# Requesting the q weights ahead of x tile 3, and four more products of zeros ahead of the first transposes

## The chip, the cores and the metric

One NeuronCore of one Trainium2 chip runs the kernel. The metric is device time in microseconds (us) of one execution, lower is better. A profiled execution also has a span, counted from the first instruction; it is about 1.7 us shorter than the time. Times inside a trace below count from the span's start.

## The reference, cut to what matters

One transformer-like block on x of 2048 rows by 512 columns (bf16): layer norm; a local, dilated attention over q, k and v; a gated feed-forward part; x plus the product of the two.

```python
xn = _layernorm(x, axis=-1)
s = _A_ref(xn, A_wqkv, A_wo)          # qkv = xn @ wqkv, attention over 8 positions, @ wo
g = _silu(_B_ref(xn, B_w_gate, B_w_up, B_w_down))
return x + s * g
```

Only the start matters here. To form the first q product the kernel needs two tiles of x (tile 0 and tile 1, 128 rows each), normalized and transposed, and the q third of wqkv.

## The kernel before

All loads are asked for by SyncE, on one queue, in the order of the program: the first four x tiles (128 KB each), then the q, k and v weights (512 KB each), then the rest.

```python
for t in range(TPQ):                  # TPQ = 4
    load_x(t)
for i in range(3):
    load_w(wqkv_sb, A_wqkv, i * D, (i + 1) * D)
load_x(TPQ, TPQ)
... # gate and up weights, further x tiles
```

While the first x tile is on its way TensorE multiplies zeros ("warm_up"), whose results nobody reads; they keep the array active. Tile 0 and tile 1 are then normalized on VectorE, transposed on TensorE into PSUM and copied to SBUF on ScalarE.

```python
warm_up(17, TQ // 2)                  # 17 products of 256 columns of zeros
first_moments(0)                      # VectorE: statistics; ScalarE: square root
first_moments(1)
first_normalize(0)
transpose(0)                          # TensorE x4, then one copy by ScalarE
first_normalize(1)
warm_up(4, P)                         # 4 products of 128 columns of zeros
transpose(1, parts=2)                 # TensorE x4, then two copies by ScalarE
warm_up(4, P)
first_moments(2)
first_moments(3)                      # needs x tile 3
first_normalize(2)                    # behind the statistics of tile 3 on VectorE
first_normalize(3)
... # 16 products for q over tiles 0 and 1; transposes of tiles 2 and 3; k, v
```

The softmax here doesn't subtract the row's maximum and nothing guards it: scores larger than these inputs give would overflow.

Of the kernel before, what the change touches and what calls it, by code (L numbers as in the profile page):

```python
# [13 lines left out]
P = 128  # L14
# [14 lines left out]
def kernel(  # L29
# [14 lines left out]
    B, S, D = A_x.shape  # L44
    DF = B_w_gate.shape[1]
    NT, NC, NF, NJ = S // P, D // P, DF // P, S // TQ
    TPQ = TQ // P
# [27 lines left out]
    wqkv_sb = wts.tile([P, NC, 3 * D], BF16, name="wqkv_sb")  # L75
# [6 lines left out]
    def load_x(t, n=1):  # L82
        nc.sync.dma_start(
            out=x_sb[:, t : t + n, :],
            in_=x2d[t * P : (t + n) * P, :].rearrange("(t p) d -> p t d", p=P),
        )

    def load_w(dst, src, lo, hi):
        nc.sync.dma_start(
            out=dst[:, :, lo:hi], in_=src.rearrange("(k p) n -> p k n", p=P)[:, :, lo:hi]  # L90
        )

    for t in range(TPQ):
        load_x(t)
    for i in range(3):
        load_w(wqkv_sb, A_wqkv, i * D, (i + 1) * D)
    load_x(TPQ, TPQ)
    for i, (lo, hi) in enumerate(((0, DF // 2), (DF // 2, DF))):
# [76 lines left out]
    def first_moments(t):  # L175
        nc.vector.bn_stats(out=stats[:, t, :], in_=x_sb[:, t, :])  # L176
        nc.vector.bn_aggr(out=mv[:, t, :], in_=stats[:, t, :])
        nc.scalar.activation(
            out=std[:, t, :], in_=mv[:, t, 1:2], func=AF.Sqrt, bias=epsc[:], scale=1.0
        )  # L180
# [39 lines left out]
    def warm_up(n, cols):  # L220

        ps = mm.tile([P, TQ], F32, name="warm_ps", tag="mm")
        for _ in range(n):
            nc.tensor.matmul(
                ps[:, 0:cols], lhsT=warm[:, 0:P], rhs=warm[:, 0:cols], start=True, stop=True
            )
# [240 lines left out]
    HT = TPQ // 2  # L467
    HQ = HT * P
    warm_up(17, TQ // 2)
    first_moments(0)  # L470
    first_moments(1)
    first_normalize(0)
# [72 lines left out]
```

## Time and profile before

| | before |
|---|---|
| time, median of 3 | 231.71 us (231.36 to 231.92) |
| span of the profiled execution | 229.8 us |
| TensorE busy | 98% |
| TensorE's share of the chain that ended last | 95% |
| first q product starts | 7.06 us |

The chain is followed back from the last instruction to whatever released it. A share of 95% for TensorE says that time can be gained elsewhere only where TensorE waits. Between its first product at 1.11 and the end of its last at 226.31, nearly all of that waiting is ahead of 7.06. The lines are in the prediction.

### The profile page before, as it was taken

Reading aid. Unit: us, or ns where it says so; the run is one execution under the profiler, and the core shown is the slowest. Engines: PE = TensorE matmul, PEld = TensorE weight load, DVE = VectorE, ACT = ScalarE, POOL = GpSimd, SP = SyncE. Lnnn points to the kernel's source line nnn. Section 1 sums busy time; section 2 is a strip of 40 time slices with the busy share of each in tenths; the row PEclk is TensorE's granted clock in tenths of the full one; section 3 lists DMA queues with packets and bytes.
Section 4 is the critical chain, followed back from the end, with each engine's and each line's share of the span. In section 5 each row is a group of like instructions: output and inputs, shape, how many; then the busy total and the mean of one; then the engine's idle time right before and its main releaser. Section 6 shows DMA issues by size and latency. Waiting matters only on the chain.

```text
span 229.8 us, 3547 instructions
## 1 busy us (share of the span) xinstructions
PE 224.7 (98%) x1339; PEld 107.6 (47%) x1339; DVE 147.5 (64%) x234; ACT 132.3 (58%) x219; POOL 20.9 (9%) x61
## 2 busy tenths in 40 slices
PE   7999999999999999999999999999999999999993
PEld 5865444444444444444444444444444444444453
DVE  5593896896995198865678169725449429945232
ACT  3779779765514867476721687646741387647211
POOL 1058924100000000110000000000000000000000
PEclk9999999999999999999999999999999999999998
DMA  6999499921288211100267611100047810000001
GB/s 156 365 374 372 109 205 200 301 81 49 85 182 198 62 27 24 26 0 0 93 163 162 146 30 23 27 11 0 27 138 160 204 30 0 0 0 4 23 23 46
DMA packets 27057, 23.71 MB, mean 103 GB/s; under 512 B 6688, under 2 KB 27040, under 8 KB 27040
## 3 DMA queue, kind: packets, MB, share of 16 engines
q1 hardware_dynamic: 27040, 23.49, 39.1%
q8 instruction: 10, 0.16, 0.3%
q14 instruction: 7, 0.06, 0.1%
HBM read 18.22 MB, written 4.21 MB: 98 GB/s over the span
## 4 chain that ended last, share of the span: by engine, by line
PE 95%; ACT 1%; DVE 1%; DMA 1%; issue 0%; DVEq 0%
PE y_ps L399 21%; PE u_ps L241 21%; PE g_ps L241 21%; PE qkv_ps L241 17%; PE s_ps L409 6%; PE L_ps L298 3%; PE o_ps L358 3%; DMA x_sb<-in_A_x_dram 1%; PE tr L207 1%; PE q_ps L241 1%; DVE stats L176 1%; ACT L383 1%; PE den_ps L318 0%; PE sp_ps L333 0%; ACT xnT L216 0%; ACT ge L383 0%
## 5 line engine op out<-in xcount | busy, mean ns | idle before, releaser
L241 PE MATMUL g_ps<-xnT,wg_sb 128*128 128x512 bf16 x224 | 57.6, 379 | 0.0
L241 PE MATMUL u_ps<-xnT,wu_sb 128*128 128x512 bf16 x224 | 57.5, 379 | 0.0
L399 PE MATMUL y_ps<-wd_sb,h 128*128 128x512 bf16 (+1 forms) x238 | 51.2, 366 | 0.0
L387 DVE TENSOR_TENSOR h<-ge,u 128x512 bf16<-128x512 bf16 x56 | 23.7, 424 | 36.6 <-ACT u L385 36.2
L287 DVE TENSOR_TENSOR pk<-q_sb,k_sb 128x2048 bf16<-128x2048 bf16 x32 | 37.8, 1220 | 8.8 <-ACT k_sb L262 8.8
L385 ACT ACTIVATE u<-u_ps 128x512 bf16<-128x512 f32 x56 | 33.5, 598 | 14.6 <-PE u_ps L241 14.5
L383 ACT ACTIVATE ge<-g_ps 128x512 bf16<-128x512 f32 x56 | 33.6, 599 | 14.0 <-PE g_ps L241 13.7
L241 PE MATMUL qkv_ps<-xnT,wqkv_sb 128*128 128x512 bf16 (+1 forms) x208 | 41.1, 355 | 0.0
L344 DVE TENSOR_TENSOR pv<-E,v_arr 128x2048 bf16<-128x2048 bf16 x32 | 38.6, 1216 | 0.0
L399 PEld LDWEIGHTS <-h 128*128 128x128 bf16 x238 | 23.3, 98 | 25.3
L406 ACT ACTIVATE sl<-y_ps 128x512 bf16<-128x512 f32 (+1 forms) x17 | 9.7, 572 | 44.0 <-PE y_ps L399 44.0
L241 PEld LDWEIGHTS <-wu_sb 128*128 128x128 bf16 x224 | 21.9, 98 | 26.6 <-issue 0.3
L241 PEld LDWEIGHTS <-wg_sb 128*128 128x128 bf16 x224 | 21.0, 98 | 26.1 <-issue 3.0
L241 PEld LDWEIGHTS <-wqkv_sb 128*128 128x128 bf16 x224 | 21.6, 98 | 19.5 <-issue 0.4
L417 DVE TENSOR_TENSOR m<-s_ps,sl 128x512 bf16<-128x512 f32 (+1 forms) x17 | 11.2, 657 | 24.2 <-PE s_ps L409 24.2
L409 PE MATMUL s_ps<-wo_sb,oT 128*128 128x512 bf16 (+1 forms) x68 | 16.6, 366 | 0.0
L192 POOL TENSOR_TENSOR rstd<-rstd,mhalf 128x1 f32<-128x1 f32 x12 | 7.7, 638 | 80.4 <-DVE rstd L189 78.2
L265 ACT ACTIVATE vst<-qkv_ps 128x512 bf16<-128x512 f32 x16 | 9.6, 597 | 6.2 <-PE qkv_ps L241 6.2
L262 ACT ACTIVATE k_sb<-qkv_ps 128x512 bf16<-128x512 f32 (+1 forms) x20 | 10.2, 516 | 3.5 <-PE qkv_ps L241 3.2
L370 DVE TENSOR_TENSOR oT<-o_ps,rb 128x1024 bf16<-128x1024 f32 x8 | 9.4, 1216 | 2.1 <-PE o_ps L358 2.1
L259 ACT ACTIVATE q_sb<-qkv_ps 128x512 bf16<-128x512 f32 (+1 forms) x16 | 8.7, 544 | 3.6 <-PE qkv_ps L241 3.3
L409 PEld LDWEIGHTS <-oT 128*128 128x128 bf16 x68 | 6.7, 98 | 7.2
(51 smaller groups left out, 120.9 us busy)
## 6 DMA issues: line engine op xcount, KB each, us to landing
v_arr<-vT SPq DMA_DIRECT2D x16, 520.0 KB, 5.2
vT<-vst SPq DMA_DIRECT2D x16, 128.0 KB, 1.7
out_dram<-o_t SPq DMA_DIRECT2D x15, 128.0 KB, 2.3
wg_sb<-in_B_w_gate_dram SPq DMA_DIRECT2D x2, 896.0 KB
wu_sb<-in_B_w_up_dram SPq DMA_DIRECT2D x2, 896.0 KB, 13.5
wd_sb<-in_B_w_down_dram SPq DMA_DIRECT2D x1, 1792.0 KB, 17.1
wqkv_sb<-in_A_wqkv_dram SPq DMA_DIRECT2D x3, 512.0 KB, 5.3
x_sb<-in_A_x_dram SPq DMA_DIRECT2D x3, 512.0 KB, 10.0
```

The source lines that it names most:

```text
L241: nc.tensor.matmul(ps, lhsT=w[:, dk, lo : lo + P], rhs=xnT[j][:, dk, i0 : i0 + n], start=(dk == 0), stop=(dk == NC - 1),)
L262: nc.scalar.activation(out=k_sb[:, c, lo : lo + n], in_=ps, func=AF.Copy)
L265: nc.scalar.activation(out=vst[:], in_=ps, func=AF.Copy)
L287: nc.vector.tensor_tensor(out=pk[:], in0=st[j]["q"][:], in1=k_sb[:, :, off : off + TQ], op=ALU.mult)
L344: nc.vector.tensor_tensor(out=pv[:], in0=st[j]["E"][:, wh, :].unsqueeze(1).to_broadcast([P, 4, TQ]), in1=st[j]["va"][:, 4 * g : 4 * g + 4, ...
L383: nc.scalar.activation(out=ge[:], in_=g_ps[:], func=AF.Gelu_apprx_tanh)
L385: nc.scalar.activation(out=u[:], in_=u_ps[:], func=AF.Copy)
L387: nc.vector.tensor_tensor(out=h[:], in0=ge[:], in1=u[:], op=ALU.mult)
L399: nc.tensor.matmul(y[:], lhsT=st[j][fc][:, tt * P : (tt + 1) * P], rhs=wd_sb[:, fc, cols], start=(fc == 0), stop=(fc == NF - 1),)
L406: nc.scalar.activation(out=sl[:, cols], in_=y[:], func=AF.Silu)
L409: nc.tensor.matmul(s[:], lhsT=st[j]["oT"][:, g, tt * P : (tt + 1) * P], rhs=wo_sb[:, g, cols], start=(g == 0), stop=(g == NC - 1),)
L417: nc.vector.tensor_tensor(out=m[:], in0=s[:], in1=sl[:, cols], op=ALU.mult)
```

## The change

The intent: let the q weights land before TensorE asks for them, and let TensorE have no idle piece between the seventeen products of zeros and the first transposes.

```diff
-    for t in range(TPQ):
+    for t in range(TPQ - 1):
         load_x(t)
-    for i in range(3):
+    load_w(wqkv_sb, A_wqkv, 0, D)
+    load_x(TPQ - 1)
+    for i in range(1, 3):
         load_w(wqkv_sb, A_wqkv, i * D, (i + 1) * D)
...
     warm_up(17, TQ // 2)
+    warm_up(4, P)
     first_moments(0)
```

## The prediction

> **What bounds the kernel now.** I read the page first: which engine is busy, then which chain ended last.
>
> ```profile
> span 229.8 us, 3547 instructions
> PE 224.7 (98%) x1339; PEld 107.6 (47%) x1339; DVE 147.5 (64%) x234; ACT 132.3 (58%) x219; POOL 20.9 (9%) x61
> ...
> PE 95%; ACT 1%; DVE 1%; DMA 1%; issue 0%; DVEq 0%
> ```
>
> TensorE is on the chain for 95% of the span; all other engines together hold about 5%. The changed code lies in the first 9 us, so the next view is the chain of waits in order of time, cut to that stretch (columns: start in us, length in us, what).
>
> ```profile
> 0.80 2.04 DMA x_sb<-in_A_x_dram
> ...
> 4.65 0.42 DVE xn L198
> 5.08 0.05 issue
> 5.12 0.61 PE tr L207 x4
> 5.73 0.43 PE warm_ps L224 x4
> 6.16 0.44 PE tr L207 x4
> 6.60 0.02 issue
> 6.62 0.39 ACT xnT L216
> 7.01 0.04 issue
> 7.06 1.91 PE q_ps L241 x16
> 8.96 0.22 PE tr L207 x4
> 9.19 0.44 PE qkv_ps L241 x4
> ```
>
> Real work on TensorE begins at 7.06. Before it: x tile 0 from memory, its statistics, its normalized copy xn (done at 5.07), the transposes of tile 0, four products of zeros, the transposes of tile 1, ScalarE's copy of the first half of tile 1. After 7.06 TensorE runs almost without a hole, so the change can gain only by moving 7.06 forward, and can lose only by moving it back or by opening a hole soon after. Last comes the timeline of the same stretch, which shows what stands beside the chain.
>
> ```profile
> 5.17 0.41 DVE L198 TENSOR_SCALAR xn<-x_sb,mv,rstd 128x512 bf16<-128x512 bf16 x1
> ...
> 6.32 0.66 DVE L176 BATCH_NORM_STATS2 stats<-x_sb 128x6 f32<-128x512 bf16 x1
> ...
> 7.01 0.36 PEld L241 LDWEIGHTS <-wqkv_sb 128*128 128x128 bf16 x4 [0.35 <-DMA wqkv_sb<-in_A_wqkv_dram]
> ...
> 7.06 0.49 PE L241 MATMUL q_ps<-xnT,wqkv_sb 128*128 128x256 bf16 x3 [0.23 <-ACT xnT L216]
> ```
>
> The reader is to see two waits that end together: the weight load had to wait for the q weights until 7.01, and the first product had to wait for ScalarE's copy, which ended at 6.62 + 0.39 = 7.01. Taking away the first alone leaves the second.
>
> One more thing decides the size: TensorE's own speed. Two lines of the groups by shape, over the first 10 us (busy us, mean ns of one, idle before and what ended it):
>
> ```profile
> L224 PE MATMUL warm_ps<-warm 128*128 128x256 bf16 x17 | 3.8, 420 | 1.1 <-DVE k_sb L161 1.1
> L241 PE MATMUL q_ps<-xnT,wqkv_sb 128*128 128x256 bf16 x16 | 1.9, 272 | 0.2 <-ACT xnT L216 0.2
> ```
>
> Same shape, 420 ns against 272. From start to start it is (3.81 - 0.42)/16 = 0.212 us for the zeros and (1.91 - 0.27)/15 = 0.109 us for q: the array ran at half speed up to some moment, which the single starts put at about 6.5 us (transposes 0.107 apart up to there, products of zeros 0.056 apart after it). The granted-clock row of the page does not show this; it reads full from the start.
>
> **What the Trainium skill says.** "TensorE: Matmul & The Clock Gate", section "Part 1: The HAM clock gate", says that the array starts at half clock and is released after a busy window of about 3.4 us, and that this window runs freely, so that its phase against the kernel's start differs from run to run. It gives start-to-start times of N / 1.2 GHz before and N / 2.4 GHz + 2.5 ns after, 213 and 109 ns for 256 columns: the trace's 0.212 and 0.109. One trace cannot show the phase; that it varies I take from the page.
>
> "DMA: Bandwidth & Descriptors", section "Queues, rings and completion order", says that on each DMA engine the descriptors of one issuing queue are consumed in ring order. So a transfer asked for earlier pushes the others back by its own length. All loads here come from one queue. The trace agrees as far as it goes: the three weight parts were asked for 0.5 us apart and landed 4.3, 5.3 and 6.3 us after their requests, one behind another.
>
> **The change part by part.** *Requests.* In the listing of instructions x tile 3 and the q weights change places; from the k weights on everything keeps its place, and the waits keep their kind. The q weights were asked for at 2.66 and landed 4.3 later, at 6.96. Now they are asked for one x request earlier (0.43 to 0.47 us), and 128 KB fewer lie ahead of them, which at the 250 to 360 GB/s of this stretch is 0.36 to 0.5 us. I expect them at 6.5 to 6.6. X tile 3 then lies behind the same 1 MB that lay ahead of the end of the q weights, so it lands near 6.96. Its statistics began at 6.32 and will begin near 7.0, 0.7 later.
>
> Does that reach TensorE? VectorE runs statistics 3 before it normalizes tile 2. Statistics 7.0 to 7.7, aggregation to 7.9, reciprocal to 8.05, xn of tile 2 done near 8.4, of tile 3 near 8.9 (after a square root on ScalarE, 0.30). TensorE takes the first at 8.80 and the second at 9.46 (starts of these transposes in its timeline). Slack of 0.4 and 0.5 us: hidden.
>
> *Four more products of zeros.* The seventeen start at 1.11 and are all fed by 1.11 + 17 x 0.212 = 4.72. Four of 128 columns at half speed take 4 x 0.107 = 0.43 and end at 5.14. The transposes may start at 5.12. So they fill the hole and cost 0.02 us at most. The added buffer of sums shifts which of the four buffers the transposes take; the only new wait is TensorE on its own seventeenth product, long done. It costs nothing.
>
> *The sum.* If the clock is released at 6.5 as in this trace: minus 0.00 for the q weights (the copy still ends at 7.01), plus 0.02 for the zeros: no change. If the clock is released before about 5.1, the twelve operations between 5.12 and 6.38 take 12 x 0.056 = 0.67 instead of 1.28; but xn of tile 1 comes at 5.58 and ScalarE's copy of tile 0 takes 0.60, so the copy of tile 1 could end near 6.5, not 7.01. The old kernel would still wait for its q weights until 7.01; the new one starts near 6.6. Then the gain is 0.45, less perhaps 0.1 because TensorE now wants xn of tile 2 at 8.3. For releases between 5.1 and 6.5 it is in between. With the phase spread evenly over 3.4 us (releases from roughly 4 to 7.4, an estimate from the page's window length), about a third of the runs gain 0.35, two fifths about 0.15, the rest nothing: 0.33 x 0.35 + 0.4 x 0.15 = 0.18 us on average. From 231.71 that makes about 231.55.
>
> **The rivals.**
> First, nothing at all: the copy and not the weights sets the start, in every run. For it: the two waits end within 0.05 us of each other. Against it: they do so in one run with one clock phase. Time: 231.7.
>
> Second, x tile 3 takes the place of the wait removed: if it lands at 7.6 or later, xn of tile 2 comes at 9.0 and TensorE waits before the second pair of transposes. For it: VectorE's order puts tile 3's statistics ahead of tile 2's normalization, and the transfer rate near 4.2 us was low. Against it: 0.4 us of slack. Time: 231.9 to 232.1.
>
> Third, the filled hole helps the clock. The idle 0.4 us between 4.72 and 5.12 is 12% of a window; if that sometimes misses the release, the new kernel is released earlier, saving up to 0.6 us before 7.06, and in phases where the old one would have stayed slow into the q products, (0.213 - 0.109) per product, up to 1.6 for sixteen. For it: the author put the zeros exactly into the hole. Against it: in this trace the window with that very hole in it was released at 6.5, and three of four executions lie within 0.4 us. Time: 231.1 in the median at best.
>
> **Range and chances.** All of these lie within 0.6 us of the time before, a quarter of one per cent; three executions of one kernel already spread over 0.56 us. I predict 231.55 us, with 231.05 to 232.0 to hold it 8 times in 10. Faster by over 2% would need 4.6 us, more than half of all the time before 7.06; slower by over 2% would need a hole that nothing in the order of instructions makes. Faster 0.01, within 2% 0.98, slower 0.01.
>
> **What would show it right or wrong.** In the profile after: the wait on the q weights before the first q product is gone, or below 0.1 us; the q weights land near 6.55; the statistics of tile 3 start near 7.0 with VectorE idle ahead of them until x lands; TensorE has no hole before the transposes of tile 2; the transposes of tile 0 start within 0.05 us of 5.12, without the 0.20 idle. The first q product starts between 6.55 (clock released early) and 7.08 (released at 6.5 or later), and every later step moves by the same amount. The prediction is wrong if that product starts later than 7.1 while the clock was up by then, if a wait for xn shows on TensorE near 8.8, or if the start moves and the end does not, which would mean that something later is tied to the transfers and not to TensorE.

## The result

| | before | after |
|---|---|---|
| median | 231.74 us (231.36 to 231.96, 6 executions) | 231.30 us (231.03 to 231.56, 6 executions) |
| ratio | 1 | 0.9984, 95% interval 0.9970 to 0.9997 |

Ratios here are the mean time of one kernel's executions over that of the other's in the same rounds, so not quite the ratio of the medians. The change gains about 0.4 us of 231.7: within 2%, but clear of zero.

The same places of the page after. TensorE still has 95% of the chain.

```profile
span 229.6 us, 3534 instructions
...
PE 95%; ACT 2%; issue 1%; DVE 0%; ACTq 0%; DVEq 0%
```

The chain of waits after, cut to the start (start us, length us, what; line numbers have moved by two or three).

```profile
1.12 4.24 PE warm_ps L226 x21
5.35 0.56 PE tr L209 x4
5.91 0.02 issue
5.93 0.91 ACT xnT L218 x2
6.84 0.04 issue
6.89 1.91 PE q_ps L243 x16
8.79 0.22 PE tr L209 x4
```

The first q product starts at 6.89 instead of 7.06, and the step ahead of it is ScalarE's copy, not the weights. The timeline shows what stands beside it.

```profile
5.29 0.35 PEld L209 LDWEIGHTS <-xn 128*128 128x128 bf16 x4 [0.20 <-DVE xn L200]
5.29 0.61 PE L209 MATMUL tr<-ident,xn 128*128 128x128 bf16 x4
...
6.60 0.10 PEld L243 LDWEIGHTS <-wqkv_sb 128*128 128x128 bf16 x1
6.89 1.91 PE L243 MATMUL q_ps<-xnT,wqkv_sb 128*128 128x256 bf16 x16 [0.25 <-ACT xnT L218]
...
6.97 0.69 DVE L178 BATCH_NORM_STATS2 stats<-x_sb 128x6 f32<-128x512 bf16 x1 [0.39 <-DMA x_sb<-in_A_x_dram]
...
7.96 0.41 DVE L200 TENSOR_SCALAR xn<-x_sb,mv,rstd 128x512 bf16<-128x512 bf16 x1
...
8.63 0.39 PE L209 MATMUL tr<-ident,xn 128*128 128x128 bf16 x4
```

The weight load is done at 6.70 and only the product waits, for ScalarE. VectorE now waits 0.39 us for x tile 3, but the normalized tile 2 is there at 8.37 and TensorE takes it at 8.63 without a wait. The transposes of tile 0 have no idle piece of TensorE in front. The chain leads from the zeros to them, because the modelled ends of the zeros reach 5.35; but their weight load waited until 5.29 for the normalized tile 0 (done at 5.23), so in this execution the zeros did not hold them up.

### The profile page after: what moved, and what is told of

Read it like the earlier page. It is cut to its first block, busy times and chain, and to the rows that moved or that the text cites. A ratio compares the mean times of both kernels' runs of the same rounds, so it can differ in the third digit from the quotient of the medians.

```text
span 229.6 us, 3534 instructions
## 1 busy us (share of the span) xinstructions
PE 223.6 (97%) x1322; PEld 107.8 (47%) x1343; DVE 147.5 (64%) x234; ACT 132.5 (58%) x219; POOL 22.2 (10%) x61
## 4 chain that ended last, share of the span: by engine, by line
PE 95%; ACT 2%; issue 1%; DVE 0%; ACTq 0%; DVEq 0%
PE y_ps L401 21%; PE u_ps L243 21%; PE g_ps L243 19%; PE qkv_ps L243 17%; PE s_ps L411 6%; PE L_ps L300 3%; PE o_ps L360 3%; PE warm_ps L226 2%; PE q_ps L243 1%; ACT u L387 1%; PE tr L209 1%; ACT xnT L218 1%; ACT L385 1%; PE den_ps L320 0%; PE sp_ps L335 0%
## 5 line engine op out<-in xcount | busy, mean ns | idle before, releaser
L243 PE MATMUL g_ps<-xnT,wg_sb 128*128 128x512 bf16 x215 | 56.6, 379 | 0.4
```

What stands on the lines that cost most here:

```text
L243: nc.tensor.matmul(ps, lhsT=w[:, dk, lo : lo + P], rhs=xnT[j][:, dk, i0 : i0 + n], start=(dk == 0), stop=(dk == NC - 1),)
```

## The experiments

Twelve runs were made, of nine different kernels, in three sets, each set on one chip; the kernel before ran as the reference in all three (11, 9 and 11 executions). Every execution counts, those near 233.5 us below too. Theory: two things gate the first q product, the landing of the q weights and ScalarE's copy of the first half of tile 1; the change moves the first, and the second comes early or late with the moment at which the array's clock is released, which differs from one execution to the next. Main rival: the zeros fill an idle piece that delays the release.

### One table for all profiles

For each profiled execution I read four moments from its trace: the release of the clock (the trace's clock record; before it, products stand 0.213 us apart for 256 columns, after it 0.109), the landing of the q weights (the last completion of that transfer), the end of ScalarE's copy of tile 1's first half, and the start of the first q product.

| run | request order | release | weights landed | copy done | first q product | span | span minus start |
|---|---|---|---|---|---|---|---|
| before | old | 6.51 | 6.96 | 7.01 | 7.06 | 229.77 | 222.71 |
| after | new | 5.92 | 6.56 | 6.84 | 6.89 | 229.59 | 222.71 |
| a_before | old | 6.09 | 6.88 | 6.83 | 6.92 | 229.63 | 222.71 |
| b_both | new | 4.52 | 6.17 | 6.63 | 6.68 | 229.39 | 222.72 |
| c_requests | new | 6.38 | 6.13 | 7.00 | 7.05 | 229.76 | 222.71 |
| d_zeros | old | 4.56 | 7.03 | 6.52 | 7.08 | 229.79 | 222.71 |
| e_hole | old | 5.38 | 6.99 | 6.56 | 7.03 | 229.75 | 222.72 |
| f_hole_filled | old | 3.95 | 7.19 | 6.60 | 7.24 | 229.97 | 222.73 |
| g_x3_later | newer | 4.11 | 6.41 | 6.50 | 6.55 | 230.75 | 224.20 |
| h_moved | new | 5.68 | 7.58 | 6.73 | 7.63 | 230.41 | 222.78 |
| i_both_again | new | 4.77 | 7.00 | 6.48 | 7.05 | 229.86 | 222.81 |
| j_requests_again | new | 3.76 | 6.52 | 6.58 | 6.63 | 229.37 | 222.74 |
| k_zeros_again | old | 6.35 | 6.72 | 6.99 | 7.04 | 229.76 | 222.72 |
| l_vector_copy | new | 4.15 | 6.51 | 6.60 | 6.65 | 229.35 | 222.71 |

Two things can be read off. In every row the first q product starts 0.04 to 0.06 us after the later of the two moments in the columns before it. And in all rows but three the rest of the kernel takes 222.71 to 222.74 us from there, whatever came before; the three are explained with their runs. So what the start gains, the end gains.

### Each part alone, the kernel before, and both

The kernel before against itself (a_before) and both parts (b_both) are the controls. c_requests leaves out the zeros:

```diff
     warm_up(17, TQ // 2)
-    warm_up(4, P)
```

d_zeros leaves out the new request order: it is the kernel before with

```diff
     warm_up(17, TQ // 2)
+    warm_up(4, P)
```

> The kernel before against itself: ratio 1.000, 231.4 to 231.9 us. If the time is set by the phase of the clock window, its own executions spread over at least 0.4 us, and those whose mean clock is 0.997 or 0.998 (the array went back to half speed before the span's end, so by the window length of 3.41 us it had been released near 6.5 or 7.0, or one window earlier) do not group with those at 1.0.

> Both parts again: ratio 0.998 to 0.999, about 231.3 us. The first q product starts between 6.55 and 7.1, in step with the release of the clock; executions with a mean clock of 1.0 are the faster ones, by about 0.3 us.

> The request order alone. My theory (the q weights and ScalarE's copy both gate the first q product, and the weights are the later one when the clock is released early): nearly the whole gain, ratio 0.9985 to 0.999, q weights landed near 6.6, statistics of tile 3 near 7.0, no wait on TensorE before the transposes of tile 2. Rival (the zeros release the clock earlier): ratio 1.000.

> The four products of zeros alone. My theory: no gain, ratio 0.9995 to 1.0005, the first q product not before 7.0 in any execution, since the q weights land at 6.96. Rival (the zeros fill a hole that delays the release of the clock): the gain of 0.0015 is here.

| run | median (range, executions) | ratio to before, 95% interval |
|---|---|---|
| before, of the set | 231.62 us (231.31 to 233.83, 11) | 1 |
| a_before | 231.53 us (231.21 to 233.46, 6) | 1.0012 (0.9970 to 1.0054) |
| b_both | 231.38 us (231.07 to 231.51, 5) | 0.9978 (0.9946 to 1.0010) |
| c_requests | 231.31 us (230.97 to 231.72, 6) | 0.9976 (0.9943 to 1.0008) |
| d_zeros | 231.49 us (231.28 to 231.73, 5) | 0.9987 (0.9955 to 1.0019) |

Three executions of the kernel before near 233.5 us (two of a_before, one of the reference) widen the intervals; the ratios of this set tell little. Its profiles tell more. In d_zeros the chain of waits no longer runs through the normalization at all:

```profile
2.66 4.37 DMA wqkv_sb<-in_A_wqkv_dram
7.03 0.05 issue
7.08 1.92 PE q_ps L241 x16
```

The clock was released early there (4.56) and the copy was done at 6.52, but TensorE stood until the weights landed at 7.03. The zeros cannot help a start that the weights set. In c_requests it is the other way round: weights at 6.13, but a late release (6.38), so that the copy came at 7.00. Its timeline:

```profile
7.05 1.91 PE L243 MATMUL q_ps<-xnT,wqkv_sb 128*128 128x256 bf16 x16 [0.25 <-ACT xnT L218]
```

Of what I expected of a_before, the spread of 0.4 us is there without the two slow ones; that executions group by their mean clock did not show cleanly (231.34, 231.45 and 231.21 us at 1.0, 231.61 at 0.997), and in b_both one at 0.997 took 231.51, one at 1.0 took 231.49.

### The rare executions near 233.5 us: idle pieces and the clock

Only the kernel before had such executions. I suspected the clock, and made its idle pieces larger. e_hole is the kernel before without the zeros behind tile 1's transposes; f_hole_filled is the same with the change's zeros in front.

```diff
     transpose(1, parts=2)
-    warm_up(4, P)
```

> The kernel before with the four zeros behind the transposes of tile 1 taken out, so that TensorE has about 0.4 us more idle time ahead of the q products. New theory for the few executions of the kernel before near 233.5 us (3 of 23, none of 22 with a part of the change): in an unlucky phase of the clock window the idle pieces near 4.9 and 6.9 us together make the window count as not busy, the release is missed by a whole window and the q products run at half speed. Then this kernel shows clearly more such executions, a quarter or more of them at 233 to 234 us, the rest at 231.5. Rival (those executions come from something else, transfers for one): as rare as before, and the median unmoved at 231.5.

> The same with the change's four zeros put ahead of the first transposes (request order as before). If missed windows are the cause, filling the first hole brings the number of executions at 233 to 234 us back down, to that of the kernel before or under it; if they come from something else, it stays with the one of the run without this filling. Median 231.5.

Measured, against 231.76 us (231.62 to 232.61, 9 executions) for before in this set: e_hole 231.55 us (231.17 to 232.20, 5), ratio 0.9993 (0.9980 to 1.0006); f_hole_filled 231.43 us (231.34 to 231.68, 5), ratio 0.9988 (0.9976 to 1.0001). None of the ten lies near 233. The timeline of e_hole shows TensorE's longer idle piece (here and in d_zeros the weight load names the weights; the product's own note names a ScalarE instruction that merely ended close by):

```profile
7.03 1.64 PEld L241 LDWEIGHTS <-wqkv_sb 128*128 128x128 bf16 x16 [1.11 <-DMA wqkv_sb<-in_A_wqkv_dram]
7.03 1.92 PE L241 MATMUL q_ps<-xnT,wqkv_sb 128*128 128x256 bf16 x16 [0.94 <-ACT std L178]
```

More idle time did not make these executions more frequent, so my expectation of a quarter or more was not met. Five executions of e_hole are weak evidence, though: if a quarter of them were of that kind, five without one would still come about one time in four (0.75^5 = 0.24). The table says more about the theory. Take the ends of the clock's windows to lie 3.41 us apart (the closing list has the working). In the four profiles without zeros in front and with a release after the first idle piece (before 6.51, a_before 6.09, c_requests 6.38, e_hole 5.38) the window's end before the release then lay at 3.09, 2.68, 2.96 and 1.96. All of these are ahead of the idle piece, which begins at 4.72 in each (the seventeenth product starts at 4.50 and takes 0.213), and the window that held it was the one that ended with the release. In no profile did the idle piece put the release off. In f_hole_filled, with a release at 3.95, TensorE stood idle for 0.53 and 1.06 us in the next 3.4 us and kept its clock.

What the three executions near 233.5 us do have in common is a mean clock of 0.993, where their neighbours have 0.997 to 1.0. Over 231.7 us that is 0.007 x 2 x 231.7 = 3.2 us at half speed. If all of it fell into TensorE's work it would cost about 1.6 of the 1.9 us that they are longer; this is an estimate and not shown. The mean also takes in half speed after TensorE's last product, where it costs nothing: in the profile of the kernel before it is 0.997 because of the last 1.40 us alone. So a longer end of the kernel is a rival that no run tests, for none of the three was profiled. All three fell into the first set, on one chip (3 of 17 executions of the kernel before, none of 16 others there). Over everything it is 3 of 43 executions of the kernel before and none of 65 of the others, too few to say whether the change has to do with it.

### x tile 3 later still

g_x3_later has both parts, and x tile 3 behind the k weights too.

```diff
     load_w(wqkv_sb, A_wqkv, 0, D)
-    load_x(TPQ - 1)
-    for i in range(1, 3):
-        load_w(wqkv_sb, A_wqkv, i * D, (i + 1) * D)
+    load_w(wqkv_sb, A_wqkv, D, 2 * D)
+    load_x(TPQ - 1)
+    load_w(wqkv_sb, A_wqkv, 2 * D, 3 * D)
```

> Both parts of the change, and x tile 3 asked for one place later still, behind the k weights as well. My theory of slack: the tile lands near 8.4 instead of 6.9 us, its statistics hold VectorE, xn of tile 2 comes near 9.8, and TensorE waits about 1.1 us before the transposes of tile 2; 232.3 to 232.5 us. Rival (order of x tile 3 does not matter, other work fills in): 231.3.

232.69 us (232.45 to 232.92, 4 executions), ratio 1.0044 (1.0028 to 1.0059). Its timeline:

```profile
8.31 0.69 DVE L178 BATCH_NORM_STATS2 stats<-x_sb 128x6 f32<-128x512 bf16 x1 [1.87 <-DMA x_sb<-in_A_x_dram]
9.31 0.41 DVE L200 TENSOR_SCALAR xn<-x_sb,mv,rstd 128x512 bf16<-128x512 bf16 x1
...
9.78 0.40 PE L209 MATMUL tr<-ident,xn 128*128 128x128 bf16 x4 [1.32 <-DVE xn L200]
```

The tile landed at 8.29, and TensorE stood 1.32 us before the transposes of tile 2. It is the row of the table with 224.20 instead of 222.71. So the slack behind x tile 3 is real and limited: the change uses up part of it, one more place and the kernel is slower than before. I had expected 1.1 us and a time of at most 232.5; it is a little more.

### The zeros between the transposes

h_moved: both parts, tile 1's transposes straight behind tile 0's.

```diff
     first_normalize(1)
-    warm_up(4, P)
     transpose(1, parts=2)
-    warm_up(4, P)
+    warm_up(6, P)
```

> Both parts, and the four zeros between the two groups of transposes moved behind the second (six there instead of four). In an execution whose clock is released after 6 us the transposes of tile 1 start near 5.7 instead of 6.0 and the first q product near 6.8 instead of 7.05; with an early release nothing changes. Mean gain against the changed kernel about 0.1 us: 231.2, so hardly to be told by time; the start of the q products in the profile, read with the moment of release, tells it.

231.35 us (231.19 to 232.15, 5 executions), ratio 0.9989 (0.9976 to 1.0002). The profiled execution was its slowest one, 232.15 us, and shows something else: the q weights took until 7.58 to land.

```profile
7.63 1.92 PE L243 MATMUL q_ps<-xnT,wqkv_sb 128*128 128x256 bf16 x16 [1.15 <-DMA wqkv_sb<-in_A_wqkv_dram]
```

On the question that it was made for it is inconclusive: copy done at 6.73 with a release at 5.68 fits the expected 6.8, but nothing came of it. What it does show is that the same request, 512 KB at 2.18 us, can land over 1 us later in one execution than in another: here at 7.58, in g_x3_later on the same chip at 6.41, in c_requests on another chip at 6.13.

### The same again on a third chip, and ScalarE's queue

i_both_again, j_requests_again and k_zeros_again repeat b, c and d. l_vector_copy takes away what makes ScalarE's copy of tile 1 late, on top of both parts: its copy of tile 0 goes to VectorE, and tile 1's transposes stand straight behind tile 0's.

```diff
-    transpose(0)
     first_normalize(1)
-    warm_up(4, P)
+    transpose(0, copy=nc.vector.tensor_copy)
     transpose(1, parts=2)
-    warm_up(4, P)
+    warm_up(6, P)
```

> Both parts, as the standard of this set: ratio 0.9975 to 0.999. With the two other sets that is more than twenty executions.

> The requests alone, again. The first try gave 0.9976 with an interval that held 1. My theory: the same ratio as both parts within 0.0007, since the zeros do not gate anything; first q product at 6.6 to 7.05 depending on the moment of release.

> The zeros alone, again. My theory: ratio 0.9993 to 1.0005 and the first q product never before the q weights' landing near 7.0. Rival (the zeros carry a part of the gain): 0.9985 or under.

> Both parts; besides, tile 1 is normalized and transposed straight behind tile 0, six zeros behind it, and VectorE, which only waits for x tile 3 there, copies tile 0's transposes, so that ScalarE's queue has tile 1 alone. If ScalarE's copy is what gates the first q product once the weights come early, that product starts near 6.5 with an early release and near 6.8 with a late one, at once after the later of the weights' landing and the copy; 0.1 to 0.3 us under both parts, 231.1 us. If the copy does not gate, the time is that of both parts.

| run | median (range, executions) | ratio to before, 95% interval |
|---|---|---|
| before, of the set | 231.58 us (231.38 to 232.08, 11) | 1 |
| i_both_again | 231.28 us (230.96 to 231.60, 6) | 0.9983 (0.9970 to 0.9996) |
| j_requests_again | 231.33 us (231.05 to 231.70, 6) | 0.9985 (0.9971 to 0.9998) |
| k_zeros_again | 231.54 us (231.35 to 232.16, 6) | 0.9998 (0.9985 to 1.0011) |
| l_vector_copy | 231.09 us (231.05 to 231.48, 6) | 0.9979 (0.9967 to 0.9991) |

This set has no execution near 233.5. The request order alone has the gain of both, the zeros alone have none that can be told from zero. The two intervals overlap, so I also took the two parts against each other: the mean of c_requests is 0.22 us under that of d_zeros, that of j_requests_again 0.31 us under that of k_zeros_again, together 0.26 us with a standard error of 0.11. The times do not exclude that the zeros have a share of the gain. j_requests_again is the favourable case: an early release (3.76) and weights at 6.52.

```profile
6.56 1.69 PEld L243 LDWEIGHTS <-wqkv_sb 128*128 128x128 bf16 x16 [0.36 <-DMA wqkv_sb<-in_A_wqkv_dram]
6.63 1.91 PE L243 MATMUL q_ps<-xnT,wqkv_sb 128*128 128x256 bf16 x16 [0.25 <-ACT xnT L218]
```

Again two waits that end together, as in the kernel before, but 0.43 us earlier. k_zeros_again had a late release (6.35) and its weights by luck at 6.72; the copy, at 6.99, set the start. My expectation that its first product would wait for weights near 7.0 missed that case; the size, no gain, was right.

i_both_again shows the other side of the new order: the q weights landed late (7.00) and x tile 3 behind them later still (7.41).

```profile
7.05 1.92 PE L243 MATMUL q_ps<-xnT,wqkv_sb 128*128 128x256 bf16 x16 [0.77 <-DMA wqkv_sb<-in_A_wqkv_dram]
7.43 0.69 DVE L178 BATCH_NORM_STATS2 stats<-x_sb 128x6 f32<-128x512 bf16 x1 [1.01 <-DMA x_sb<-in_A_x_dram]
...
8.89 0.23 PEld L209 LDWEIGHTS <-xn 128*128 128x128 bf16 x4 [0.21 <-DVE xn L200]
```

Here TensorE did wait for the normalized tile 2, and the row's last column is 222.81, 0.1 us over the others; h_moved, with 222.78, is the same case. The slack of x tile 3 is thin in executions with late transfers.

l_vector_copy has the lowest median of all, 0.19 us under both parts of the same set, but the two intervals lie over each other, so it is not shown to beat the changed kernel. It does beat the kernel before. Its timeline:

```profile
6.21 0.66 ACT L218 ACTIVATE xnT<-tr 128x256 bf16<-128x256 bf16 x2 [1.18 <-PE tr L209]
6.56 1.72 PEld L243 LDWEIGHTS <-wqkv_sb 128*128 128x128 bf16 x16 [0.22 <-DMA wqkv_sb<-in_A_wqkv_dram]
6.65 1.91 PE L243 MATMUL q_ps<-xnT,wqkv_sb 128*128 128x256 bf16 x16
```

ScalarE now sits idle for 1.18 us until tile 1's transposes are there, so its queue is no longer what delays the copy. With an early release that gained nothing (6.65 against 6.63 in j_requests_again): normalizing tile 1 ends at 5.73 and is the next gate. A late release, where I expected more, was not caught in a profile of it.

## Why the prediction was right or wrong

The time, 231.30 us, lies inside the range, in the class that was given 0.98; the gain is about twice the one predicted.

- *Two waits that end together; taking away one alone does not help where the copy is late.* Right. c_requests, weights at 6.13 and copy at 7.00, starts at 7.05, as late as the kernel before.
- *The q weights land at 6.5 to 6.6, x tile 3 near 6.96.* Right for the profiled execution: 6.56 and 6.94. Over all profiles it is a spread and not a moment: 6.13 to 7.58 for the weights in the new place, 6.72 to 7.19 in the old one.
- *Statistics of tile 3 near 7.0, xn of tile 2 near 8.4, no wait on TensorE.* Right: 6.97, 8.37, and no wait. g_x3_later shows the wait that would have come with a landing at 8.29, i_both_again the start of it at 7.41.
- *The zeros cost 0.02 us at most and gain nothing.* Right in time (k_zeros_again 0.9998), and the idle piece before the first transposes is gone in the profile after. With an early release it is not: the zeros are then through sooner, and 0.15 us (d_zeros), 0.27 (b_both) or 0.53 (f_hole_filled) stay idle. The transposes started at 5.29, not within 0.05 us of 5.12, because x tile 0 landed at 3.01 instead of 2.84, which has nothing to do with the change's zeros.
- *The gain comes in executions with an early release, up to 0.45 us.* Right as far as profiles show it: j_requests_again starts at 6.63, 0.45 before the 7.08 of d_zeros, both with an early release.
- *The average of 0.18 us.* This term was mis-sized: the measured gain of the first comparison is 0.0016 x 231.7 = 0.37 us, with an interval of 0.07 to 0.70, and the other four ratios with both parts or the requests alone lie at 0.9976 to 0.9985 (those of b_both and c_requests with intervals that hold 1). Two readings show where the sum was short. I gave a third of the executions an early release (before 5.1); seven of the fourteen profiles have one, six more lie before 6.5, and with these shares my own sum gives 0.24 us, though seven of fourteen may be chance. And I worked the gain out against the start of the one profiled execution, 7.06, as if every old execution had its weights at 6.96, but took it off the median. The profiled execution took 231.51 us, less than the median of 231.71. Taken off 231.51, the same 0.18 would have given 231.33. A time less 231.51 - 7.06 = 224.45 estimates the start; the median of 40 executions of the kernel before (without the three near 233.5) is 231.63 us, a start near 7.2. f_hole_filled is an execution of this kind: old order, weights at 7.19, start at 7.24, 231.68 us. A landing at 7.19 is later than the latest copy in any profile (7.01), so it sets the start whatever the release; my sum left such executions out. That late weights hold up the unprofiled executions too is not shown.
- *The rivals.* That nothing moves fell with b_both and j_requests_again (6.68 and 6.63). That x tile 3 takes the place of the wait is true only one place further, or in an execution with slow transfers. That the zeros help the clock has nothing to stand on: k_zeros_again has 0.9998, and in no profile without the zeros did the idle piece put the release off (above). More profiles with the zeros have an early release (six of nine, against one of five); so few can fall that way by the chance of the phase. And where the weights set the start, as in d_zeros, an early release alone gained nothing.

## What to carry to other kernels

Where two waits end within 0.05 us of each other, ask what moves each of them from one execution to the next; a change to one of them is worth the average over executions, not what one profile shows. In a kernel bound by one engine after a short start, the moment at which that engine's real work begins shows, in each profile, which of the waits set it. A handful of profiles does not measure the mean gain, though: the six starts in the old order have a mean of 7.06, the seven in the new order (6.63 to 7.63, g_x3_later left out) one of 6.94, 0.12 us less, where the times say about 0.4. And ask how the profiled execution lies among the others before taking a gain off a median. And a request moved ahead is paid by the one it overtakes: look for the consumer's slack first, and for the engine that runs in order behind it.

## What the Trainium skill lacked or had wrong

- "TensorE: Matmul & The Clock Gate", the table in Part 1, has the full clock come after a busy window of about 3.4 us. The runs agree with a window of that length (in thirteen of the fourteen traces the fall-back after TensorE's last product comes 225.280 us after the release, 66 windows of 3.413 us; in that of the kernel before 221.866 us, 65 windows; the two differ by 3.414), and with the freely varying phase (releases from 3.76 to 6.51 us). But the window need not be busy throughout: in j_requests_again the release at 3.76 us came 2.64 us after the first product at 1.12.
- The same page, Part 4, says that the full clock does not engage for transposes and gives about 275 ns for one in a kernel. Here the transposes (nc.tensor.transpose in the kernel) sped up with the release like all else, from 0.107 to 0.056 us from start to start. Their durations, whose ends are modelled, go from 314 to 219 ns. The groups by shape of the first 10 us show it, for d_zeros with its early release and then for the kernel before:

```profile
L207 PE MATMUL tr<-ident,xn 128*128 128x128 bf16 x16 | 1.6, 220 | 0.2 <-DVE xn L198 0.2
```

```profile
L207 PE MATMUL tr<-ident,xn 128*128 128x128 bf16 x16 | 2.0, 265 | 0.2 <-DVE xn L198 0.2
```

- "DMA: Bandwidth & Descriptors" gives fixed costs and rates, but no spread from execution to execution. For the same 512 KB request behind three x tiles the landing ranged from 6.13 to 7.58 us in eight profiles of five kernels on three chips or more; the end of ScalarE's copy ranged from 6.48 to 7.01 in all fourteen.
- No page has it: the profile's granted-clock row reads full speed from the span's start, though the products of zeros stood 0.213 us apart until the release. The distance between starts shows the clock there, the row does not.
